# The decay table on ScalarE's DMA queue, and scores taken four chunks ahead instead of three, in a retention layer followed by two MLPs

## The chip, the cores and the metric

The kernel runs on one core of a Trainium2 chip. Its engines work side by side: TensorE (PE) multiplies matrices, VectorE (DVE) and ScalarE (ACT) work elementwise, GpSimd (POOL) does small elementwise work, SyncE (SP) issues DMA loads and stores. Each engine runs its own instructions in order and waits on semaphores for others. ACT can issue DMAs too, on a queue of its own. The metric is the device time of one execution in microseconds (us); before the change the median of 3 runs is 589.42 us (588.61 to 590.28).

## The reference

Two batches, 8 heads, 768 positions, 64 channels per head. With positions cut into blocks, a decay `lam` per head, `Dmask[i, j] = lam ** (i - j)` for i >= j and 0 otherwise:

```
for each block:
    intra = (q k^T * Dmask) v
    inter = (q * lam ** (pos + 1)) kv_state
    out   = intra + inter
    kv_state = lam ** block * kv_state + (k * lam ** (block - 1 - pos))^T v
x = out as 1536 tokens x 512
h = x @ w_in (2048 wide);  x = (max(h, 0) + alpha * min(h, 0)) @ w_out
h = x @ w_in2;             out = max(h, 0) ** 2 @ w_out2
```

All of it is f32. The reference's block is 64; the kernel uses 128, which gives the same result.

## The kernel before

**Retention.** The work is cut into 12 chunks (`NN`): 6 blocks of 128 positions by 2 batches, a chunk being one block of one batch with all 8 heads, the batches in turn. For chunk n the function names are those of the steps: `scores(n)` puts k^T q into PSUM (tile `s`); `decay(n)` multiplies it on DVE by the decay table `dec` into SBUF (`sc`); `outputs(n)` accumulates `sc` times `v` (line 459) and, from the second block on, the state times `q` (line 467) in PSUM (`o`), and makes the state's increment `pk` (line 477); `factors(n)` scales `q` by `grow` and `r` (the k rows) by `dec` on POOL; `keep_output` casts `o` to the high part `xah` on ACT; `keep_rest` makes the low part `xal`: up to chunk 8 PE subtracts the high part from `o` in PSUM (line 495) and ACT casts the rest, from chunk 9 (`RESTS`) on DVE subtracts (line 493). Only then is the `o` bank free; there are two. `keep_state` updates the state on DVE and scales it on ACT (`old`).

**The decay table.** `dec` holds, for 128 rows, 8 heads and 128 columns, powers of lam, shifted by one per row. DVE computes one strip of powers per head (`z`, 8 x 256), SP stores it to DRAM (`zd`), and a second DMA reads it back into 128 partitions with a step of one element per partition: 1024 pieces of 512 bytes. In the kernel before both DMAs are on SP's queue, and chunk 1's `v` load is held until POOL has copied one column of `dec` (line 305). `growth()` makes `grow` from the same strip with four matmuls.

**What sets the order.** All is written out by hand, and each engine runs its part in the order of the calls. Loads (`load_qk`, `load_vk`, 256 KB a tile) are issued by SP. The head takes the scores of `FIRST` = 4 chunks before any output; the first `FIRST - 2` are copied to SBUF by ACT, as `scores` has only two PSUM buffers. Between, `keep_warm` runs matmuls on zeros. Then the loop over chunks runs outputs(n), decay(n + 2), factors(n + 2), scores(n + 3) and the keeping of chunk n. DMA completion semaphores are used in turn, eight in all, so a DMA waits for the one eight places before it.

**The MLPs.** Weights come as f32 pieces of 512 KB (`raw`) and are split on ACT and DVE into a high part `wh` and a low part `wl`, a unit per piece: `start` (two ACT instructions, lines 122 and 123), `begin` (three on DVE, 129 to 131), `middle` (DVE line 139, then ACT's cast, line 141), `end` (DVE line 150). Five units run inside the retention loop (`EARLY_UNITS`), the others in the MLP's steps. A step makes `h` (line 172, 12 matmuls), activates it (`g`, high part `gh`, low part `gl`), and two steps later PE multiplies `gh` and `gl` by the second weights (line 225 or 227, 12 matmuls).

Of the kernel before, what the change touches and what calls it, by code (L numbers as in the profile page):

```python
# [7 lines left out]
F32 = mybir.dt.float32  # L8
# [7 lines left out]
B, H, S, D = 2, 8, 768, 64  # L16
CH = 128
NCH = S // CH
NN = B * NCH
NPAIR = H // 2  # L20
# [5 lines left out]
CPT = TT // CH  # L26
ZW = 256
RESTS = 9
FIRST = 4
LA = 3  # L30
DA = 2
AHEAD = 3
EARLY = 4
# [11 lines left out]
EARLY_UNITS = [0, 0, 0, 1, 0, 1, 0, 1, 0, 1, 1, 0]  # L45
# [8 lines left out]
def retention_then_two_mlps(  # L54
# [15 lines left out]
    nc = tc.nc  # L70
# [34 lines left out]
    def load_piece(queue=nc.scalar):  # L105
        if len(loaded) < 4 * NF:
            j = SEQ[len(loaded)]
            loaded.append(j)
            raws[j] = raw = rawp.tile([128, DM, 2], U32, tag="raw", name=f"raw{j}")
            w = (w1, w2)[j // (2 * NF)]  # L110
            queue.dma_start(raw.rearrange("p a b -> p (a b)"), w[j % (2 * NF)])
# [42 lines left out]
    conv = Conversion()  # L154
# [114 lines left out]
    actx = ExitStack()  # L269
    ap1 = actx.enter_context(tc.tile_pool(name="ap1", bufs=1))  # L270
    ap2 = actx.enter_context(tc.tile_pool(name="ap2", bufs=2))
    qp = actx.enter_context(tc.tile_pool(name="qp", bufs=LA + 4))
    kp = actx.enter_context(tc.tile_pool(name="kp", bufs=LA + 2))
    scp = actx.enter_context(tc.tile_pool(name="scp", bufs=LA + 1))

    psc = actx.enter_context(tc.tile_pool(name="psc", bufs=2, space=PSUM))
    pso = actx.enter_context(tc.tile_pool(name="pso", bufs=2, space=PSUM))
# [17 lines left out]
    def load_qk(n):  # L295
        q_t = qp.tile([128, NPAIR, CH], F32, tag="q", name=f"q{n}")
        k_t = kp.tile([128, NPAIR, CH], F32, tag="k", name=f"k{n}")
        nc.sync.dma_start(k_t, kt[n])
        nc.sync.dma_start(q_t, qt[n])
        qk_t[n] = q_t, k_t  # L300

    def load_vk(n):
        v_t = kp.tile([128, H, D], F32, tag="v", name=f"v{n}")
        if n == 1:
            nc.gpsimd.tensor_copy(v_t[:, 0, 0:1], dec[:, 0, 0:1])
        nc.sync.dma_start(v_t, vr[n])
        r_t = None
        if ORDER[n][0] < NCH - 1:
            r_t = kp.tile([128, H, D], F32, tag="r", name=f"r{n}")
            nc.sync.dma_start(r_t, kr[n])  # L310
        vk_t[n] = v_t, r_t
# [5 lines left out]
    def keep_warm(i):  # L317
        pw = pso.tile([128, NPAIR, CH], F32, tag="o", name=f"warm_ps{i}")
        for a in range(WARM[i]):
            nc.tensor.matmul(pw[:, a % NPAIR, :], warm, warm, start=True, stop=True)  # L320
# [20 lines left out]
        nc.gpsimd.tensor_copy(head[:, :, t], m)  # L341

    keep_warm(0)
    for n in range(FIRST):
        load_qk(n)

    nc.vector.tensor_copy(sq[:, 0:1], lam_sb)
# [8 lines left out]
    a, p = sq[:, 0 : NB - 1], sq[:, 1:NB]  # L356
# [31 lines left out]

    zd = dram.tile([H, ZW], F32, name="zd")
    dec = ap1.tile([128, H, CH], F32, name="dec")  # L390
    nc.sync.dma_start(zd, z)
    load_vk(0)
    nc.sync.dma_start(dec, bass.AP(zd[:, :].tensor, zd[:, :].offset, [[1, 128], [ZW, H], [1, CH]]))
    dec_v = dec.rearrange("p (a t) i -> p t a i", t=2)

    grow = ap1.tile([128, NPAIR, CH], F32, name="grow")

    def growth():
        pg = psk.tile([128, 2, NPAIR, D], F32, tag="pk", name="pg")
        pg = pg.rearrange("p a b c -> p (a b c)").rearrange("p (a i) -> p a i", i=CH)  # L400
        for a in range(NPAIR):
            nc.tensor.matmul(
                pg[:, a], head[:, a].rearrange("h t d -> h (t d)"), z[:, CH:ZW], start=True,
                stop=True,
            )
        nc.vector.tensor_copy(grow, pg)
# [7 lines left out]
    sc_t = {}  # L414

    def scores(n):
        q_t, k_t = qk_t[n]
        ps = psc.tile([128, 2, NPAIR, CH], F32, tag="s", name=f"s{n}")
        for a in range(NPAIR):
            for t in range(2):  # L420
                rows = slice(t * D, (t + 1) * D)
                nc.tensor.matmul(  # L422
                    ps[:, t, a, :], k_t[rows, a, :], q_t[rows, a, :], start=True, stop=True
                )
        sc = scp.tile([128, 2, NPAIR, CH], F32, tag="sc", name=f"sc{n}")
        if n < FIRST - 2:
            nc.scalar.copy(sc, ps)
            ps = sc
        sc_t[n] = sc, ps

    def decay(n):
        sc, ps = sc_t[n]
        for a in [slice(0, 2), slice(2, 4)] if n == 0 else [slice(0, 4)]:
            nc.vector.tensor_tensor(sc[:, :, a], ps[:, :, a], dec_v[:, :, a], ALU.mult)  # L434

# [14 lines left out]
    def outputs(n):  # L450
        c, b = ORDER[n]
        q_t = qk_t.pop(n)[0]
        v_t, r_t = vk_t.pop(n)
        sc = sc_t.pop(n)[0]
        po = pso.tile([128, NPAIR, CH], F32, tag="o", name=f"o{n}")

        for a in range(NPAIR):
            for t in range(2):
                nc.tensor.matmul(  # L459
                    po[t * D : (t + 1) * D, a, :], v_t[:, 2 * a + t, :], sc[:, t, a, :],  # L460
                    start=a == 0, stop=c == 0, skip_group_check=True,
                )
        if c > 0:
            for a in range(NPAIR):
                for t in range(2):
                    d = slice(t * D, (t + 1) * D)
                    nc.tensor.matmul(  # L467
                        po[d, a, :], state[b, c % 2][d, a, :], q_t[d, a, :], start=False,
                        stop=True, skip_group_check=True,
                    )  # L470
        pk = None
        if c < NCH - 1:
            pk = psk.tile([128, 2, NPAIR, D], F32, tag="pk", name=f"pk{n}")[:, 0]
            for a in range(NPAIR):
                for t in range(2):
                    h = 2 * a + t
                    nc.tensor.matmul(  # L477
                        pk[t * D : (t + 1) * D, a, :], r_t[:, h, :], v_t[:, h, :], start=a == 0,
                        stop=True, skip_group_check=True,
                    )  # L480
        return po, pk

    def keep_output(n, po):
        ti, cols = n // CPT, slice((n % CPT) * CH, (n % CPT + 1) * CH)
        xh, xl = xt[ti]
        nc.scalar.copy(xh[:, :, cols], po)

    def keep_rest(n, po):

        ti, cols = n // CPT, slice((n % CPT) * CH, (n % CPT + 1) * CH)  # L490
        xh, xl = xt[ti]
        if n >= RESTS:
            nc.vector.tensor_tensor(xl[:, :, cols], po, xh.bitcast(F32)[:, :, cols], ALU.subtract)
            return
        nc.tensor.matmul(po, less, xh[:, :, cols], start=False, stop=True, skip_group_check=True)  # L495
        nc.scalar.copy(xl[:, :, cols], po)

    def keep_state(n, pk):
        c, b = ORDER[n]
        new = state[b, (c + 1) % 2]  # L500
        if c > 0:
            nc.vector.tensor_tensor(new, pk, old_t[n], ALU.add)
        else:
            nc.scalar.copy(new, pk)
        if c < NCH - 2:
            old_t[n + B] = old = ap2.tile([128, NPAIR, D], F32, tag="old", name=f"old{n}")
            for a in range(NPAIR):
                nc.scalar.activation(
                    old[:, a, :], new[:, a, :], AF.Copy, scale=grow[:, a, CH - 1 : CH]
                )  # L510

    for n in range(FIRST):
        scores(n)
        if n == 2:
            growth()
    keep_warm(1)
    load_vk(1)
    for n in range(2):
        factors(n)
    for n in range(DA):  # L520
        decay(n)
    for n in range(NN):
        if n + FIRST < NN:
            load_qk(n + FIRST)
        if n + 2 < NN:
            load_vk(n + 2)
        if EARLY_LOADS[n]:
            load_piece(nc.sync)
        if n == 0:
            nc.sync.dma_start(alpha_sb, alpha)  # L530
        po, pk = outputs(n)
        if n + DA < NN:
            decay(n + DA)
        if EARLY_UNITS[n]:
            conv.begin()
        keep_output(n, po)
        if pk is not None:
            keep_state(n, pk)
        if EARLY_UNITS[n]:
            conv.middle(load=False)  # L540
            conv.end()
        if n + 1 < NN and EARLY_UNITS[n + 1] or n == NN - 1:
            conv.start(conv.k)
        if n + 2 < NN:
            factors(n + 2)
        if FIRST <= n + LA < NN:
            scores(n + LA)
        keep_rest(n, po)
    actx.close()
    psum["mlp"] = ctx.enter_context(  # L550
        tc.tile_pool(name="psum", bufs=1, space=PSUM, reuse_waits="tile")
# [12 lines left out]
    for s in range(len(steps) + LAG):  # L564
        if s < len(steps):
            m, t, f, part = steps[s]
# [78 lines left out]
```

## Time and profile before

| what | value |
|---|---|
| median of 3 runs | 589.42 us |
| profiled execution | 591.76 us, its span 590.0 us |
| PE busy in the span | 578.9 us (98%) |
| DVE, ACT, POOL busy | 360.1, 296.7, 28.3 us |
| mean granted clock of PE | 0.994 of full |
| decay table, issue to landing | 9.75 to 16.19 us |
| first output matmul | 17.03 us |
| first MLP matmul | 63.49 us |

The span runs from the first to the last instruction; the execution's time is 1.8 us longer. A busy share is an average over stages with different limits: here PE is full for nearly the whole span, and what isn't full lies in the first 64 us and the last 4. The granted clock is a share of full speed (2.4 GHz); 0.5 is the lower level, 1.2 GHz.

### The profile page before, as it was taken

To read this page: it belongs to the slowest core of one execution; us is meant where nothing else is said; L and a number is where in the kernel's file an instruction comes from. 1 tells how busy PE (TensorE), PEld (TensorE's weight loads), DVE (VectorE), ACT (ScalarE), POOL (GpSimd) and SP (SyncE) were. 2 spreads that over 40 slices of the span, in tenths; PEclk is the share of its full clock that TensorE was granted. 3 is DMA by queue.
4 is the path that set the end of the run, shared out by engine and by line. 5 is a ranking of instruction groups with operands and counts; after the bars stand their busy time and mean duration, and the time that the engine had idled before them with its cause. 6 is when DMAs were issued, how large, how long until landed. Compare 5 with 4: busy or idle time off the path is not lost.

```text
span 590.0 us, 7970 instructions
## 1 busy us (share of the span) xinstructions
PE 578.9 (98%) x3069; PEld 479.9 (81%) x3069; DVE 360.1 (61%) x616; ACT 296.7 (50%) x515; POOL 28.3 (5%) x31
## 2 busy tenths in 40 slices
PE   8799899999999999999999999999999999999997
PEld 7688788888888888888888888888888888888885
DVE  4489897577578777887887787577522222222422
ACT  2476777566556766576576565555522222321220
POOL 1565000000000000000000000000000000000000
PEclk9799999999999999999999999999999999999999
DMA  6895334332436223233232132332100000400401
GB/s 215 284 390 187 107 112 142 139 108 96 167 130 213 77 103 108 96 118 108 106 111 104 41 139 74 141 107 73 73 0 1 0 1 0 143 0 1 142 1 72
DMA packets 25733, 62.39 MB, mean 106 GB/s; under 512 B 2904, under 2 KB 3936, under 8 KB 25696
## 3 DMA queue, kind: packets, MB, share of 16 engines
q1 hardware_dynamic: 17632, 32.53, 15.7%
q10 hardware_dynamic: 8064, 29.36, 14.5%
q8 instruction: 24, 0.39, 0.3%
q14 instruction: 13, 0.11, 0.1%
HBM read 52.44 MB, written 9.45 MB: 105 GB/s over the span
## 4 chain that ended last, share of the span: by engine, by line
PE 96%; DMA 2%; DVE 1%; issue 0%; DVEq 0%
PE h L172 44%; PE acc L227 22%; PE acc L225 22%; PE o L459 2%; PE o L467 2%; PE s L422 2%; PE pk L477 1%; DMA dec<-zd 1%; PE o L495 1%; DVE sc L434 0%; DMA zd<-z 0%; DMA lam_sb<-in_lam_dram 0%; DVE err L367 0%; DVE sq L349 0%; DVE ps L241 0%
## 5 line engine op out<-in xcount | busy, mean ns | idle before, releaser
L191 ACT CAST gh<-g 128x512 fp32r<-128x512 f32 x96 | 59.7, 621 | 92.6 <-DVE g L182 38.6
L182 DVE SCALAR_TENSOR_TENSOR g<-h,g 128x512 f32<-128x512 f32 x48 | 33.2, 691 | 117.3 <-ACT g L181 117.3
L181 ACT ACTIVATE g<-h 128x512 f32<-128x512 f32 x48 | 28.7, 597 | 124.9 <-PE h L172 124.9
L196 DVE TENSOR_TENSOR gl<-g,gh 128x512 fp32r<-128x512 f32 x96 | 66.5, 692 | 31.0 <-ACT gh L191 22.3
L172 PE MATMUL h<-xah,wl 128*128 128x512 f32 x192 | 74.8, 390 | 0.0
L172 PE MATMUL h<-xah,wh 128*128 128x512 f32 x192 | 74.7, 389 | 0.0
L172 PE MATMUL h<-xal,wh 128*128 128x512 f32 x192 | 74.7, 389 | 0.0
L225 PE MATMUL acc<-gh,wl 128*128 128x512 f32 x192 | 74.7, 389 | 0.0
L225 PE MATMUL acc<-gh,wh 128*128 128x512 f32 x192 | 74.7, 389 | 0.0
L225 PE MATMUL acc<-gl,wh 128*128 128x512 f32 x192 | 74.7, 389 | 0.0
L172 PE MATMUL h<-xbh,wl 128*128 128x512 f32 x192 | 74.7, 389 | 0.0
L172 PE MATMUL h<-xbl,wh 128*128 128x512 f32 x192 | 74.7, 389 | 0.0
L172 PE MATMUL h<-xbh,wh 128*128 128x512 f32 x192 | 74.7, 389 | 0.0
L227 PE MATMUL acc<-wl,gh 128*128 128x512 f32 x192 | 74.7, 389 | 0.0
L227 PE MATMUL acc<-wh,gh 128*128 128x512 f32 x192 | 74.7, 389 | 0.0
L227 PE MATMUL acc<-wh,gl 128*128 128x512 f32 x192 | 74.7, 389 | 0.0
L186 DVE SCALAR_TENSOR_TENSOR g<-h,g 128x512 f32<-128x512 f32 x42 | 29.0, 691 | 41.7 <-ACT g L185 41.6
L150 DVE TENSOR_TENSOR wl<-bits,wh 128x512 fp32r<-128x512 f32 x64 | 44.8, 699 | 3.9 <-ACT wh L141 3.8
L131 DVE SCALAR_TENSOR_TENSOR bits<-raw,bits 128x512 uint32<-128x512 uint32 x64 | 45.1, 704 | 2.2
L139 DVE CUSTOM_DVE_ANT_0 bits<-raw,bits 128x1024 uint16<-128x1024 uint16 x64 | 45.1, 705 | 0.1
L122 ACT ACTIVATE bits<-raw 128x512 f32<-128x512 f32 x64 | 43.1, 674 | 0.0
L123 ACT ACTIVATE raw<-raw 128x512 int32<-128x512 uint32 x64 | 42.8, 669 | 0.0
(81 smaller groups left out, 824.0 us busy)
## 6 DMA issues: line engine op xcount, KB each, us to landing
raw<-in_w_dram ACTq DMA_DIRECT2D x56, 512.0 KB, 3.2
ps<-sums SPq DMA_DIRECT2D x24, 256.0 KB, 3.2
sums<-p SPq DMA_DIRECT2D x20, 256.0 KB, 2.2
raw<-in_w_dram SPq DMA_DIRECT2D x8, 512.0 KB, 6.0
k<-in_kt_dram SPq DMA_DIRECT2D x12, 256.0 KB, 5.7
q<-in_qt_dram SPq DMA_DIRECT2D x12, 256.0 KB, 5.4
v<-in_vr_dram SPq DMA_DIRECT2D x12, 256.0 KB, 6.0
r<-in_kr_dram SPq DMA_DIRECT2D x10, 256.0 KB, 5.3
```

Source lines behind the costliest of these rows:

```text
L122: nc.scalar.activation(x.bitcast(F32), high.bitcast(F32), AF.Abs)
L123: nc.scalar.activation(low.bitcast(I32), low, AF.Copy, scale=2.0**-29)
L131: nc.vector.scalar_tensor_tensor(x, high, 0xC0000000, x, ALU.bitwise_and, ALU.bitwise_or)
L139: nc.vector.tensor_tensor(x.bitcast(I32), x.bitcast(I32), low.bitcast(I32), ALU.add)
L150: nc.vector.tensor_tensor(lo, x, hi.bitcast(F32), ALU.subtract)
L172: nc.tensor.matmul(ph, w[:, cols], x[:, c, :], start=c == 0 and i == 0, stop=c == NC - 1 and i == 2)
L182: nc.vector.scalar_tensor_tensor(g, ph, 0.0, g, ALU.max, ALU.mult)
L186: nc.vector.scalar_tensor_tensor(g, ph, 0.0, g, ALU.max, ALU.subtract)
L191: nc.scalar.copy(gh, g)
L196: nc.vector.tensor_tensor(gl, g, gh.bitcast(F32), ALU.subtract)
L225: nc.tensor.matmul(acc[t][i], w[:, cols], g, **flags)
L227: nc.tensor.matmul(acc[t][i], g[:, cols], w, **flags)
```

## The change

The table's DMA moves from SP's queue to ACT's: a new function `tables()` holds `growth()` and the DMA, and is called after the scores of chunk 1. SP's queue goes on behind the strip's store with v0, r0, k4, q4, v1, r1, k5, q5; POOL's copy that held v1 is gone. `FIRST` goes from 4 to 5 and `LA` from 3 to 4: the head takes five chunks' scores, the first four copied to SBUF by ACT, and the loop takes scores four chunks ahead. Buffers follow: `q` from 7 to 9, `k`, `v` and `r` from 5 to 6, `sc` from 4 to 5, and `sc` is now reserved in `decay` where ACT made no copy. In the loop, the rest of a chunk that takes no scores (chunks 0 and 8) is put off until after the next chunk's outputs; from chunk 9 on the rest stands right behind the state, ahead of the weight unit's `middle`, and in chunk 10 ahead of `begin` too.

```diff
-FIRST = 4
-LA = 3
+FIRST = 5
+LA = 4
...
     def load_vk(n):
         v_t = kp.tile([128, H, D], F32, tag="v", name=f"v{n}")
-        if n == 1:
-            nc.gpsimd.tensor_copy(v_t[:, 0, 0:1], dec[:, 0, 0:1])
         nc.sync.dma_start(v_t, vr[n])
...
+    def tables():
+
+        growth()
+        nc.scalar.dma_start(
+            dec, bass.AP(zd[:, :].tensor, zd[:, :].offset, [[1, 128], [ZW, H], [1, CH]])
+        )
+
     nc.sync.dma_start(zd, z)
     load_vk(0)
-    nc.sync.dma_start(dec, bass.AP(zd[:, :].tensor, zd[:, :].offset, [[1, 128], [ZW, H], [1, CH]]))
-    dec_v = dec.rearrange("p (a t) i -> p t a i", t=2)
+    load_qk(FIRST - 1)
+    load_vk(1)
+    load_qk(FIRST)
...
     for n in range(FIRST):
         scores(n)
-        if n == 2:
-            growth()
+        if n == 1:
+            tables()
     keep_warm(1)
-    load_vk(1)
...
         po, pk = outputs(n)
+        for x in pending:
+            keep_rest(*x)
+        pending = []
         if n + DA < NN:
             decay(n + DA)
-        if EARLY_UNITS[n]:
+        if EARLY_UNITS[n] and n < NN - 2:
             conv.begin()
         keep_output(n, po)
         if pk is not None:
             keep_state(n, pk)
+        if n >= RESTS:
+            keep_rest(n, po)
         if EARLY_UNITS[n]:
+            if n >= NN - 2:
+                conv.begin()
             conv.middle(load=False)
             conv.end()
...
         if FIRST <= n + LA < NN:
             scores(n + LA)
-        keep_rest(n, po)
+            keep_rest(n, po)
+        elif n < RESTS:
+            pending = [(n, po)]
```

The head on SP's queue, before, from the strip's store on (a name's first number is the chunk, the last a buffer):

```order
L391 DMA zd_212<-z_118 8x256
L306 DMA v0_215<-in_vr_dram 128x512
L310 DMA r0_217<-in_kr_dram 128x512
L393 DMA dec_213<-zd_212 128x8x128
L306 DMA v1_284<-in_vr_dram 128x512
L310 DMA r1_287<-in_kr_dram 128x512
L298 DMA k4_295<-in_kt_dram 128x512
L299 DMA q4_294<-in_qt_dram 128x512
```

And ACT's queue now, from the first copy of scores on:

```order
L435 COPY sc0_245<-s0_236 128x1024
L435 COPY sc1_256<-s1_247 128x1024
L394 DMA dec_213<-zd_212 128x8x128
L435 COPY sc2_274<-s2_265 128x1024
L435 COPY sc3_285<-s3_276 128x1024
```

The table's DMA has left SP's row of loads and stands on ACT between the copies of chunk 1 and chunk 2; SP's loads follow the strip's store without it.

PE now, from the table's matmuls `pg` to chunk 2's outputs; before, `s4` (the scores of chunk 4) stood behind `pk1`:

```order
L410 MATMUL pg_258<-z_118,head_134 128x128 x4
L430 MATMUL s2_265<-q2_166,k2_167 128x128 x8
L430 MATMUL s3_276<-q3_170,k3_171 128x128 x8
L430 MATMUL s4_287<-q4_219,k4_220 128x128 x8
L318 MATMUL warm_ps1_296<-warm_126 128x128 x10
L470 MATMUL o0_321<-sc0_245,v0_215 64x128 x8
L488 MATMUL pk0_330<-v0_215,r0_217 64x64 x8
L470 MATMUL o1_359<-sc1_256,v1_223 64x128 x8
L488 MATMUL pk1_368<-v1_223,r1_225 64x64 x8
L506 MATMUL o0_321<-xah0_84,less_132 128x512
L430 MATMUL s5_389<-q5_227,k5_228 128x128 x8
L506 MATMUL o1_359<-xah0_84,less_132 128x512
```

Chunk 4's scores have moved ahead of the warm-up matmuls, and chunk 0's rest behind chunk 1's outputs.

DVE at the end of the retention stage, before, from chunk 9's state on (`bits4` and `bits3` are the weight units of chunks 9 and 10):

```order
L502 TENSOR_TENSOR state1_1_224<-pk9_828,old7_734 128x256
L139 ISA bits4_791<-raw4_641,bits4_791 128x1024
L150 TENSOR_TENSOR wl4_846<-bits4_791,wh4_844 128x512
L493 TENSOR_TENSOR xal2_89<-o9_811,xah2_88 128x4x128
L129 TENSOR_SCALAR bits3_848<-bits3_848 128x512
L130 TENSOR_SCALAR bits3_848<-bits3_848 128x512
L131 SCALAR_TENSOR_TENSOR bits3_848<-raw3_760,bits3_848 128x512
L139 ISA bits3_848<-raw3_760,bits3_848 128x1024
L150 TENSOR_TENSOR wl3_879<-bits3_848,wh3_877 128x512
L493 TENSOR_TENSOR xal2_89<-o10_855,xah2_88 128x4x128
L493 TENSOR_TENSOR xal2_89<-o11_884,xah2_88 128x4x128
```

and now:

```order
L513 TENSOR_TENSOR state1_1_235<-pk9_826,old7_744 128x256
L504 TENSOR_TENSOR xal2_89<-o9_809,xah2_88 128x4x128
L139 ISA bits4_801<-raw4_654,bits4_801 128x1024
L150 TENSOR_TENSOR wl4_848<-bits4_801,wh4_846 128x512
L504 TENSOR_TENSOR xal2_89<-o10_856,xah2_88 128x4x128
L129 TENSOR_SCALAR bits3_850<-bits3_850 128x512
L130 TENSOR_SCALAR bits3_850<-bits3_850 128x512
L131 SCALAR_TENSOR_TENSOR bits3_850<-raw3_769,bits3_850 128x512
L139 ISA bits3_850<-raw3_769,bits3_850 128x1024
L150 TENSOR_TENSOR wl3_881<-bits3_850,wh3_879 128x512
L504 TENSOR_TENSOR xal2_89<-o11_885,xah2_88 128x4x128
```

Each remainder `xal2` has moved up: chunk 9's ahead of line 139, chunk 10's ahead of the whole unit of `bits3`. On PE, chunk 8's rest now stands between `pk9` and `o10`, and there are no scores in chunk 8.

## Rows read from the trace of the kernel before

**Rows 1.** The page, DMA issues: count, KB each, median us to landing.

```profile
raw<-in_w_dram ACTq DMA_DIRECT2D x56, 512.0 KB, 3.2
...
q<-in_qt_dram SPq DMA_DIRECT2D x12, 256.0 KB, 5.4
```

**Rows 2.** Windows: length, busy PE, PEld, DVE, ACT, POOL, PEclk, DMA share, GB/s.

```profile
10.00:14.00 4.00, 4.00 (x43) 3.64 (x41) 0.69 (x1) 0.00 (x0) 0.00 (x0) 1.00 0.84 231
14.00:16.00 2.00, 0.85 (x8) 0.66 (x6) 0.00 (x0) 0.00 (x0) 0.00 (x0) 1.00 0.04 7
...
17.80:24.70 6.90, 6.21 (x65) 5.53 (x67) 4.04 (x4) 3.74 (x11) 3.10 (x4) 0.51 0.96 321
...
63.50:586.10 522.60, 522.53 (x2306) 432.35 (x2304) 317.26 (x533) 265.26 (x443) 0.00 (x0) 1.00 0.25 87
```

**Rows 3.** Timeline of the head: start us, us, engine, line, tile, [idle before, releaser].

```profile
8.74 0.43 SPq L310 DMA_DIRECT2D r<-in_kr_dram  x1
8.95 1.01 ACT L427 COPY sc<-s 128x1024 f32<-128x1024 f32 x1 [1.36 <-PE s L422]
...
12.35 2.50 PE L320 MATMUL warm_ps<-warm 128*128 128x128 f32 x20
...
16.29 3.29 DVE L434 TENSOR_TENSOR sc<-sc,dec 128x512 f32<-128x512 f32 x3 [4.23 <-DMA dec<-zd]
...
17.03 0.66 PE L459 MATMUL o<-sc,v 128*64 128x128 f32 x8 [2.18 <-DVE sc L434]
...
18.50 1.12 PE L459 MATMUL o<-sc,v 128*64 128x128 f32 x8 [0.80 <-DVE sc L434]
...
25.76 1.09 PE L459 MATMUL o<-sc,v 128*64 128x128 f32 x16
```

**Rows 4.** Chain that ended last, in order of time: start us, us.

```profile
9.75 6.44 DMA dec<-zd
```

**Rows 5.** DMA of 183 to 188 us: queue's packets, MB, share; issue's landing.

```profile
q1 hardware_dynamic: 530, 0.95, 55.8%
...
raw<-in_w_dram ACTq DMA_DIRECT2D x1, 512.0 KB, 5.1
```

**Rows 6.** Timeline of PE, chunk 8 to the first MLP matmul.

```profile
50.87 1.09 PE L459 MATMUL o<-sc,v 128*64 128x128 f32 x16
51.90 1.09 PE L467 MATMUL o<-q,state 64*64 64x128 f32 x16
52.92 0.69 PE L477 MATMUL pk<-v,r 128*64 128x64 f32 x16
53.53 1.16 PE L422 MATMUL s<-q,k 64*128 64x128 f32 x16
54.63 0.51 PE L495 MATMUL o<-xah,less 128*128 128x512 f32 x1
55.06 1.09 PE L459 MATMUL o<-sc,v 128*64 128x128 f32 x16
...
61.45 1.09 PE L459 MATMUL o<-sc,v 128*64 128x128 f32 x16 [1.76 <-issue]
...
63.49 0.50 PE L172 MATMUL h<-xah,wl 128*128 128x512 f32 x1
```

**Rows 7.** Timeline of DVE around the end of the retention stage.

```profile
60.67 0.68 DVE L493 TENSOR_TENSOR xal<-o,xah 128x512 fp32r<-128x512 f32 x1
61.27 0.42 DVE L129 TENSOR_SCALAR bits<-bits 128x512 f32<-128x512 f32 x1
...
69.74 0.69 DVE L196 TENSOR_TENSOR gl<-g,gh 128x512 fp32r<-128x512 f32 x1
```

**Rows 8.** Timeline of ACT in the same stretch.

```profile
53.51 0.58 ACT L496 CAST xal<-o 128x512 fp32r<-128x512 f32 x1
...
61.05 0.57 ACT L486 CAST xah<-o 128x512 fp32r<-128x512 f32 x1
```

**Rows 9.** Timeline of PE, first use of `gl` in the MLP.

```profile
72.24 0.39 PE L225 MATMUL acc<-gl,wh 128*128 128x512 f32 x1
```

More of the change, by code (lines that the diff above doesn't have):

```diff
@@ L271, in retention_then_two_mlps @@
     ap2 = actx.enter_context(tc.tile_pool(name="ap2", bufs=2))
-    qp = actx.enter_context(tc.tile_pool(name="qp", bufs=LA + 4))
-    kp = actx.enter_context(tc.tile_pool(name="kp", bufs=LA + 2))
-    scp = actx.enter_context(tc.tile_pool(name="scp", bufs=LA + 1))
+    qp = actx.enter_context(tc.tile_pool(name="qp", bufs=FIRST + 4))
+    kp = actx.enter_context(tc.tile_pool(name="kp", bufs=FIRST + 1))
+    scp = actx.enter_context(tc.tile_pool(name="scp", bufs=FIRST))
     psc = actx.enter_context(tc.tile_pool(name="psc", bufs=2, space=PSUM))
@@ L343, in retention_then_two_mlps @@
     keep_warm(0)
-    for n in range(FIRST):
+    for n in range(FIRST - 1):
         load_qk(n)
@@ L390, in retention_then_two_mlps @@
     dec = ap1.tile([128, H, CH], F32, name="dec")
+    dec_v = dec.rearrange("p (a t) i -> p t a i", t=2)
+    def tables():
[3 more added lines that the diff above has]
+        )
     nc.sync.dma_start(zd, z)
     load_vk(0)
-    nc.sync.dma_start(dec, bass.AP(zd[:, :].tensor, zd[:, :].offset, [[1, 128], [ZW, H], [1, CH]]))
-    dec_v = dec.rearrange("p (a t) i -> p t a i", t=2)
+    load_qk(FIRST - 1)
+    load_vk(1)
+    load_qk(FIRST)
     grow = ap1.tile([128, NPAIR, CH], F32, name="grow")
@@ L424, in scores @@
                 )
-        sc = scp.tile([128, 2, NPAIR, CH], F32, tag="sc", name=f"sc{n}")
-        if n < FIRST - 2:
+        if n < FIRST - 1:
+            sc = scp.tile([128, 2, NPAIR, CH], F32, tag="sc", name=f"sc{n}")
             nc.scalar.copy(sc, ps)
             ps = sc
-        sc_t[n] = sc, ps
+        sc_t[n] = ps
     def decay(n):
-        sc, ps = sc_t[n]
+        ps = sc = sc_t[n]
+        if n >= FIRST - 1:
+            sc = scp.tile([128, 2, NPAIR, CH], F32, tag="sc", name=f"sc{n}")
+        sc_t[n] = sc
         for a in [slice(0, 2), slice(2, 4)] if n == 0 else [slice(0, 4)]:
@@ L453, in outputs @@
         v_t, r_t = vk_t.pop(n)
-        sc = sc_t.pop(n)[0]
+        sc = sc_t.pop(n)
         po = pso.tile([128, NPAIR, CH], F32, tag="o", name=f"o{n}")
@@ L521, in retention_then_two_mlps @@
         decay(n)
+    pending = []
     for n in range(NN):
-        if n + FIRST < NN:
-            load_qk(n + FIRST)
+        if n + FIRST + 1 < NN:
+            load_qk(n + FIRST + 1)
         if n + 2 < NN:
@@ L531, in retention_then_two_mlps @@
         po, pk = outputs(n)
+        for x in pending:
+            keep_rest(*x)
+        pending = []
         if n + DA < NN:
             decay(n + DA)
-        if EARLY_UNITS[n]:
+        if EARLY_UNITS[n] and n < NN - 2:
             conv.begin()
```

## The prediction

> **What bounds the kernel now.** I read four views in this order. The table of windows came first, to find where TensorE (PE) is not busy. From 63.5 us to the end of the matmuls PE is busy for 522.53 of 522.60 us [rows 2]: the two MLPs are a solid block, and the change doesn't touch them. So the time can only move in the first 63.5 us, or by PE waiting inside the block. Then the timeline and the chain of waits of the head: the chain's longest piece that isn't a matmul is the decay table `dec`, issued at 9.75 and landed 6.44 us later, at 16.19 [rows 4]. VectorE (DVE) sits 4.23 us until then, PE has run out of warm-up matmuls at 14.85, and the first `o` matmul starts at 17.03, 0.84 us behind the table; its second half waits another 0.80 us for DVE [rows 3]. The gap costs twice: in 17.8 to 24.7 us the granted clock is 0.51 of full, the 1.2 GHz level [rows 2], and chunk 2's outputs begin only at 25.76 [rows 3]. From there a chunk takes PE a steady 4.19 us with no wait, until a gap of 1.76 us ahead of chunk 11's outputs, and `h`, the first matmul of the MLP, starts at 63.49 [rows 6]. Last I looked at the rows of DVE and ScalarE (ACT) around that end: PE takes the first `gl` at 72.24 [rows 9], and DVE made it at 69.74 to 70.43 [rows 7], so there is 1.8 us of slack.
>
> **The table's new queue.** ACT is in order, and issues the table behind the copy of chunk 1's scores, which ends at 8.95 + 1.01 = 9.96 [rows 3]; before, SP issued it at 9.75. Issue costs 0.2 us, then. What matters is what it shares. Before, only v0 and r0 stood ahead of it, and nothing behind: v1's load waits for POOL's copy, itself waiting for the table. Now SP issues k4, q4 at 9.2 and 9.6 (0.43 us apart, behind r0 at 8.74 [rows 3]) and then v1, r1, k5, q5, k6, q6, v2 without a stop. No row shows two queues filled at 10 us, so I bound the landing. From below: a 512 KB load on ACT's queue alone takes 3.2 us [rows 1], 13.2 us. From above: all nine of these loads go first, 9 x 0.262 MB at the 321 GB/s of the crowded stretch is 7.3 us, and the table's own 0.52 MB at the 231 GB/s of its stretch 2.3 us [rows 2]: 19.6 us. The nearest row is the weight load that ACT issues in 183 to 188 us, where SP's queue moves 0.95 MB of older loads: 5.1 us to landing [rows 5] against 3.2 alone. It was held up by 1.9 us, about what the older loads had left to move, not by twice its own length or more. At 10 us the older loads (rest of v0 and r0, k4, q4) are at most 1.05 MB, 3.3 us by 321 GB/s; 9.96 + 3.3 + 3.2 gives 16.5, and less if v0 is partly gone. I take 16.2, as before, and keep 13.2 and 19.6.
>
> The Trainium skill ("DMA: Bandwidth & Descriptors", section on queues, rings and completion order) says that each DMA engine goes round between the queues it has work for, a packet at a time, and its rules for kernel authors say that spreading loads over SP and ACT doesn't give bandwidth. By the first the table would also share with loads issued after it, and land near the upper bound; that is the last rival below. The row at 183 us leans to the older loads alone, but there nothing was issued behind.
>
> **The head's sum.** Score matmuls of chunk 4 fill PE from q4's landing: q4 is issued at 9.6; those 1.05 MB at 321 GB/s give 12.9, about 13.4 with a little for the receipt. Then 1.10 us of scores [rows 6] and 2.50 of warm-up [rows 3] end at 17.0, so that PE has no gap before the first outputs but about 1 us at 12.4 to 13.4, and I expect the clock to hold. From the table on: 0.84 to the first output and 0.80 for DVE's second half, as before; then at full clock two `o` (1.03 each), two `pk` (0.61), one `s` (1.10), two `rest` (0.43) [rows 6], together 5.24. Chunk 2 begins at 16.19 + 0.84 + 0.80 + 5.24 = 23.1 instead of 25.76: **2.7 us gained**. ACT's two extra copies (1.01 each) lie while it is idle, and decay of chunks 2 and 3 now reads SBUF, off the path. POOL loses the little copy. r2's load is next late: SP's DMAs take their semaphores in turn, and r2's is the table's, so r2 and all loads behind it wait for the table to land. They have some 7 us until chunk 2's `pk`. Against that the loads no longer pause: in 14 to 16 us the DMA moved 7 GB/s [rows 2]; I cost the wait at nothing, and at up to 2 us if the table is late.
>
> **The tail's sum**, on the clock of before. Chunk 8 has no scores any more: 1.10 us less (they ran in the head). The gap of 1.76 goes, since the remainder of chunk 9 now stands on DVE ahead of the weight unit's middle. That makes 2.86. Two waits come instead. `o9` follows `pk8` at once, but takes chunk 7's bank, which ACT empties at 53.51 + 0.58 = 54.09, when PE could start at 53.53: 0.6. And `o10` takes chunk 8's, whose rest matmul now stands right ahead of it: 0.51 of matmul, 0.58 of cast and a little to signal, 1.2 in place of the 0.43 that the step took: 0.75 [rows 6, 8]. PE reaches `h` 1.5 us earlier. But DVE doesn't: chunk 10's unit used to begin at 61.27, and now waits behind chunk 10's remainder, so behind the cast xah10. That is at 61.05 in ACT's order [rows 8], 0.61 later now since DVE's remainder (60.67 to 61.27 [rows 7]) moved ahead of the conversion that ACT waits for: 61.66, its end 62.24, plus the remainder's 0.61: the unit begins at 62.9, 1.6 later. All that follows on DVE and ACT up to the first `gl` is back to back, so `gl` ends near 72.0 instead of 70.43. PE wants it at 72.24 - 1.5 = 70.7 and stands 1.3 us. **Tail: 0.2 us gained**, between 1.5 (the unit is not late) and -0.8 (DVE one contended instruction later).
>
> Sum: 2.7 + 0.2 = 2.9 us off the profiled execution's 591.76, 588.9. That execution is 2.34 us above the runs' median of 589.42; at the median's level this is **586.5 us**. Its own range, with the table 1 us either way and the tail's bounds, is 584.9 to 588.0.
>
> **Rivals.**
> - The tail pays: DVE's unit isn't pushed back, and the 1.3 us stand doesn't appear: 585.2. For it: DVE and ACT have idle stretches there; against it: the wait on xah10 is in the order itself. Chance 0.12.
> - The clock or the fifth scores eat the gain. q4 may land as the page's median load, 5.4 us after issue [rows 1], at 15.0; scores and warm-up then end at 18.6 and chunk 2 starts near 23.9, a gain of 1.9. But PE would have stood for 2.6 us from 12.4, more than the 2.2 us before the clock fell to 1.2 GHz. At that level the way from first output to chunk 2 took 25.76 - 17.03 = 8.73 us [rows 3], so from 17.0 nothing is gained: 589.2 with the tail's 0.2. Chance 0.25, with times of 588 to 589.5.
> - Slower: the table shares with every load that SP issues after it. One mechanism, at 10 to 19 us: decay, the factors of POOL and all outputs start late, and PE stands between 17.0 and the table. From a landing of about 18.4 on, the gap is the 2.2 us after which the clock fell. At 18.8: 18.8 + 0.84 + 8.73 = 28.4, 2.6 later than now, less 0.2: 591.8. Chance 0.18. That the change doesn't bring the table sooner at all is already in the forecast.
>
> **How the numbers follow.** Forecast 0.45, the rivals 0.12, 0.25, 0.18. A measurement of this kernel tells about 0.3% (1.8 us) from no change, so faster means below 587.7. Nearly all of the forecast, the tail rival and a small part of the second count as faster: 0.57; most of the second as the same: 0.25; the last and a little more as slower: 0.18. The range leaves a tenth at either side: 584.8 to 591.2.
>
> **What would show it.** The table's landing in the chain of waits: about 16, right if 15 to 17. The granted clock in 14 to 25 us: 1.00 throughout. Chunk 2's first output (line 470) near 23. Loads without a pause at 14 to 16. At the end: the gap before chunk 11's outputs gone, one of about 0.75 before chunk 10's, and PE standing at the first down-projection (line 225) for `gl`. The forecast is wrong if the table lands past 18, if the clock halves before 25, or if PE reaches the second MLP step without a stand.

## The result and the profile after

The changed kernel is slower: 596.0 us (median of 4 runs, 595.51 to 597.6) against 589.01 us for the kernel before (4 runs, 587.95 to 590.28). The ratio is 1.0108, with a 95% interval of 1.0075 to 1.0141. The forecast was 586.5.

| us | before | after |
|---|---|---|
| profiled execution | 591.76 | 595.93 |
| its span | 590.0 | 593.9 |
| decay table landed | 16.19 [rows 4] | 20.89 |
| first output matmul `o0` | 17.03 [rows 3] | 21.73 |
| chunk 2's outputs | 25.76 [rows 3] | 29.79 |
| `h`, first matmul of the MLP | 63.49 [rows 6] | 66.55 |

The profiled execution of before is one of its slower ones, 2.75 us above its median, so the two profiles differ by only 4.2 us where the medians differ by 7.0. Within the pair, everything is lost ahead of chunk 2: its outputs start 4.03 us later, and from there to the end of the span it takes 564.2 us before and 564.1 after.

The chain of waits of after (start us, us, what) has the table as its longest piece ahead of the MLP, as before [rows 4], but much longer, with DVE's five decay multiplications behind it:

```profile
9.65 11.24 DMA dec<-zd
...
20.99 8.37 DVE sc L445 x5
```

The timeline of after's head, PE's row (start us, us, engine, line, tile, idle before and its releaser), answers to [rows 3]:

```profile
15.02 1.16 PE L430 MATMUL s<-q,k 64*128 64x128 f32 x16 [3.31 <-DMA q<-in_qt_dram]
16.11 2.50 PE L318 MATMUL warm_ps<-warm 128*128 128x128 f32 x20
21.73 0.66 PE L470 MATMUL o<-sc,v 128*64 128x128 f32 x8 [3.12 <-DVE sc L445]
23.19 0.66 PE L470 MATMUL o<-sc,v 128*64 128x128 f32 x8 [0.81 <-DVE sc L445]
...
29.79 1.09 PE L470 MATMUL o<-sc,v 128*64 128x128 f32 x16
```

PE stands twice: 3.31 us for q4 ahead of the fifth scores, then 3.12 us for the table, after the warm-up has ended at 18.61. Windows of after (length, busy PE, PEld, DVE, ACT, POOL, PEclk, DMA share, GB/s), beside [rows 2]:

```profile
10.00:14.00 4.00, 1.71 (x32) 1.51 (x28) 0.45 (x1) 1.93 (x2) 0.00 (x0) 1.00 1.05 312
14.00:16.00 2.00, 0.98 (x16) 1.00 (x16) 0.00 (x0) 0.00 (x0) 0.00 (x0) 1.00 1.05 350
...
23.00:28.00 5.00, 4.16 (x57) 3.81 (x57) 5.00 (x4) 2.02 (x6) 5.00 (x3) 0.66 0.99 280
23.90:27.20 3.30, 2.65 (x36) 2.49 (x33) 3.30 (x2) 2.02 (x6) 3.30 (x3) 0.50 1.03 281
63.50:586.10 522.60, 522.07 (x2337) 431.67 (x2336) 318.77 (x535) 267.57 (x447) 0.00 (x0) 1.00 0.25 87
```

The loads indeed no longer pause: 350 GB/s in 14 to 16 us, where it was 7 [rows 2]. The bytes are there, but they aren't the table's. The drop to the 1.2 GHz level is still there, only later and shorter: 0.50 in 23.9 to 27.2 us, where it was 0.51 in 17.8 to 24.7 [rows 2]. DVE is busy for all of 23 to 28 us, and the chain above goes through DVE up to 29.4 (20.99 + 8.37): PE now waits for decay too. The last row shows that the MLPs are untouched.

The DMA queues of after (packets, MB, share of 16 engines; q1 is SP's, q10 ACT's) in 9 to 12, 12 to 16, 16 to 18, 18 to 20 and 20 to 21 us, where 9 to 12 has no row for q10:

```profile
q1 hardware_dynamic: 437, 0.80, 97.2%
...
q1 hardware_dynamic: 487, 0.90, 63.4%
q10 hardware_dynamic: 818, 0.42, 39.1%
...
q1 hardware_dynamic: 376, 0.68, 91.6%
q10 hardware_dynamic: 184, 0.09, 16.3%
...
q1 hardware_dynamic: 276, 0.49, 66.4%
q10 hardware_dynamic: 34, 0.02, 2.9%
...
q1 hardware_dynamic: 13, 0.02, 5.7%
q10 hardware_dynamic: 4, 0.00, 0.6%
```

This is the central reading. The table is 1024 packets of 512 bytes, 0.52 MB. None of it moves before 12 us, at least 2.3 us after its issue at 9.65. Then it gets 0.42 MB in 4 us while SP's queue gets 0.90. By 18 us 0.02 MB is left, and this little takes until 20.89. The Trainium skill ("DMA: Bandwidth & Descriptors", section on queues, rings and completion order) says that an engine goes round its queues a packet at a time. The trace agrees in so far as both queues move in the same 4 us; that the turn goes by packets it doesn't show, as 818 packets of ACT's queue went beside 487 of SP's.

That loads issued after the table were served ahead of its end is seen from v1 and q6 (timeline of SP: start us, us; then the DMA issues: KB, us to landing):

```profile
10.00 0.43 SPq L304 DMA_DIRECT2D v<-in_vr_dram  x1
14.18 0.33 SPq L299 DMA_DIRECT2D q<-in_qt_dram  x1
...
v<-in_vr_dram SPq DMA_DIRECT2D x1, 256.0 KB, 6.0
q<-in_qt_dram SPq DMA_DIRECT2D x1, 256.0 KB, 6.4
```

v1 landed at 16.0 and q6 at 20.6. They were issued 0.35 and 4.5 us after the table, which landed at 20.89.

At the other end of the stage two of the forecast's three waits are there. Timeline of PE, then DVE, of after, beside [rows 6, 7]:

```profile
62.46 1.09 PE L470 MATMUL o<-sc,v 128*64 128x128 f32 x16 [0.68 <-ACT xal L507]
...
66.55 0.50 PE L172 MATMUL h<-xah,wl 128*128 128x512 f32 x1
75.56 0.50 PE L225 MATMUL acc<-gh,wl 128*128 128x512 f32 x1 [0.54 <-ACT gh L191]
...
75.54 0.69 DVE L196 TENSOR_TENSOR gl<-g,gh 128x512 fp32r<-128x512 f32 x1
```

The gap of 1.76 us ahead of chunk 11's outputs [rows 6] is gone; 0.68 us ahead of chunk 10's outputs and 0.54 us at the first down-projection have come.

### The profile page after: what moved, and what is told of

Read it like the earlier page. It is cut to its first block, busy times and chain, and to the rows that moved or that the text cites. A ratio compares the mean times of both kernels' runs of the same rounds, so it can differ in the third digit from the quotient of the medians.

```text
span 593.9 us, 7958 instructions
## 1 busy us (share of the span) xinstructions
PE 579.0 (97%) x3069; PEld 479.4 (81%) x3069; DVE 361.6 (61%) x616; ACT 298.6 (50%) x517; POOL 30.5 (5%) x30
## 3 DMA queue, kind: packets, MB, share of 16 engines
q1 hardware_dynamic: 16592, 32.01, 15.5%
HBM read 52.44 MB, written 9.45 MB: 104 GB/s over the span
## 4 chain that ended last, share of the span: by engine, by line
PE 93%; DVE 2%; DMA 2%; ACT 2%; issue 0%; POOL 0%; POOLq 0%; DVEq 0%; ACTq 0%
PE h L172 43%; PE acc L225 22%; PE acc L227 22%; DMA dec<-zd 2%; DVE sc L445 1%; PE o L478 1%; PE o L470 1%; PE s L430 1%; PE warm_ps L318 1%; PE pk L488 1%; PE o L506 1%; ACT sc L435 0%; ACT bits L122 0%; ACT raw L123 0%; ACT xah L497 0%
## 5 line engine op out<-in xcount | busy, mean ns | idle before, releaser
L225 PEld LDWEIGHTS acc<-gh,wl 128*128 128x128 f32 x192 | 36.1, 188 | 8.4 <-ACT gh L191 1.0
```

Source lines behind the costliest of these rows:

```text
L225: nc.tensor.matmul(acc[t][i], w[:, cols], g, **flags)
```

## The experiments

Two things in the change lie ahead of the first output: the table's queue, and the fifth scores, which PE must do in order, before the warm-up and `o0`. The first theory after the result was that the queue alone does it (S in the expectations). That the fifth scores do it too (P) came up when e1 had missed the time that S gave. The two were taken apart in four kernels: the change itself (both), e1 (all of the change but the queue; "scores" below), f2 (queue only) and f3 (neither, but SP's loads issued early as in the change). Every ratio is against runs of the kernel before on the same chip, with its 95% interval; the medians of before in the three sets of runs were 589.47, 589.05 and 589.77 us.

**e1_table_on_sp**: the changed kernel, the table back on SP ahead of k4.

```
 def tables():
     growth()
-    nc.scalar.dma_start(dec, ...)
...
 load_vk(0)
+nc.sync.dma_start(dec, bass.AP(zd[:, :].tensor, ...))
 load_qk(FIRST - 1)
```

> The changed kernel with one part undone: the table's DMA goes back to SP's queue, behind v0 and r0 and ahead of k4, q4, v1, r1, k5, q5. Nothing else differs from the changed kernel. Theory S (sharing): on its own queue the table shares the DMA engines piece by piece with loads that are issued after it, 512 bytes of its own against 2048 of theirs; on the loads' queue it keeps its turn. Then it lands at 15 to 17 us as in the kernel before (16.2) instead of 20.9, chunk 2's first output starts at 22.5 to 24.5 instead of 29.8, and the time is 5 to 7 us under the changed kernel's 596, at 588 to 590. Theory B (bytes in flight): any loads issued behind the table slow it, whatever queue; then it lands at 19 or later and the time stays within 2 us of 596.

Measured: 594.62 us, 1.0093 [1.0074, 1.0111]. Timeline of PE in e1 (the table landed 7.2 us after its issue):

```profile
18.07 2.08 PE L428 MATMUL s<-q,k 64*128 64x128 f32 x16 [6.17 <-DMA q<-in_qt_dram]
20.08 3.11 PE L318 MATMUL warm_ps<-warm 128*128 128x128 f32 x20
23.12 1.09 PE L468 MATMUL o<-sc,v 128*64 128x128 f32 x16
28.04 1.09 PE L468 MATMUL o<-sc,v 128*64 128x128 f32 x16
```

The table lands in 7.2 us instead of 11.2, at 16.6, as theory S had it. But the 588 to 590 us that S gave for it don't come: almost nothing is gained. (Theory B had the time right, and the table wrong, at 19 or later.) PE now stands 6.17 us for q4, which is behind the table; the fifth scores take 2.08 us where after took 1.16, the clock having fallen meanwhile, and the warm-up 3.11 instead of 2.50. The first output comes at 23.12, later than after's 21.73, though the table had long been there. So the queue isn't all: with the table back on SP, the rest of the change costs nearly as much.

**f3_sp_s4_in_loop**: the kernel before with SP's loads issued early and without the hold on v1, table on SP, fifth scores back in the loop. **f2_act_s4_in_loop**: the same, but the table on ACT's queue, behind chunk 1's copy. The loop's loads move to `load_qk(n + FIRST + 2)` and the buffers grow to 9 and 6 in both.

```
 load_vk(0)
 nc.sync.dma_start(dec, ...)        # f3; f2: nc.scalar.dma_start at n == 1 of the scores loop
+load_qk(FIRST)
+load_vk(1)
+load_qk(FIRST + 1)
...
-    if n == 1:
-        nc.gpsimd.tensor_copy(v_t[:, 0, 0:1], dec[:, 0, 0:1])
```

> As f2_act_s4_in_loop, but with the table on SP's queue behind v0 and r0 and ahead of k4. The fourth corner: neither the sharing nor the fifth scores. P and S both: the table lands at 15 to 17, the first output 0.84 later, chunk 2 at 22 to 24, the time within 1 us of before. If the earlier loads as such are dear (theory B), the time is 2 us or more above before.

> The loads of the changed kernel (table on ACT's queue beside k4, q4, v1, r1, k5, q5, k6, q6, v2, no hold, its buffers for q, k, v, r) with four chunks' scores ahead, three in the loop and the end as in the kernel before. It leaves the sharing alone and takes the fifth scores out of PE's way. Theory S: the table lands at 19.5 to 21.5 as in the changed kernel, the first output 0.84 later, chunk 2 at 27 to 29, the time 592 to 595. Theory P alone (the whole price is the fifth scores): the first output at 17 or earlier, the time within 1 us of before.

Measured: f3 589.41 us, 1.0001 [0.9985, 1.0017]; f2 595.26 us, 1.0095 [1.0076, 1.0114]. The two differ in nothing but the table's queue, and its place with it: 5.9 us. f3 came as expected but for chunk 2, 0.3 us late; f2 is as S had it, though chunk 2 and the time are each a little beyond the range given. f3, timeline of PE (the table landed 6.3 us after its issue):

```profile
16.84 0.66 PE L460 MATMUL o<-sc,v 128*64 128x128 f32 x8 [2.01 <-DVE sc L435]
...
24.32 1.09 PE L460 MATMUL o<-sc,v 128*64 128x128 f32 x16
```

f2, the same (the table landed 10.9 us after its issue):

```profile
11.80 2.50 PE L318 MATMUL warm_ps<-warm 128*128 128x128 f32 x20
21.67 1.12 PE L459 MATMUL o<-sc,v 128*64 128x128 f32 x8 [7.38 <-DVE sc L434]
29.86 0.33 PE L459 MATMUL o<-sc,v 128*64 128x128 f32 x2
```

f2, window of 17.8 to 24.7 us (columns as above, the clock third from the end):

```profile
17.80:24.70 6.90, 2.68 (x30) 2.29 (x32) 3.77 (x3) 0.40 (x1) 3.73 (x3) 0.50 0.72 249
```

On ACT's queue the table takes 10.9 us without the fifth scores in the head, 11.2 with them, and PE here stands 7.38 us for it. The clock is at the 1.2 GHz level throughout the window. In after the same time was filled with the fifth scores, their wait and the warm-up, which ended at 18.61, so that the first output waited for the table alone, and both begin chunk 2 near 29.8. On SP's queue, ahead of the same loads, it takes 6.3, and the kernel is as fast as before. The four cells: neither 1.0001, queue 1.0095, scores 1.0093, both 1.0108. Each of the two costs nearly everything by itself, since PE waits for the later of q4's work and the table; undoing one changes less than the intervals can tell, undoing both gains all of it. The cells aren't simply parts of the change, though: in e1 the table stands ahead of q4 on SP's queue, and PE gets q4 at 18.07, in after at 15.02. The change with the loads behind q4 held back until the table has landed would show what the fifth scores are worth with both in time; it was not run.

**e3_act_with_hold**: the kernel before, only the table moved to ACT's queue, v1 still held until it lands.

```
-nc.sync.dma_start(dec, ...)
...
     scores(n)
+    if n == 1:
+        nc.scalar.dma_start(dec, ...)
```

> The kernel before with the table's DMA alone moved to ACT's queue, behind the copy of chunk 1's scores; POOL's copy still holds v1's load, so that only v0 and r0 are in flight beside it. S: it lands at 15 to 17 us and the time is within 1 us of before. Theory Q (the queue itself): a table of 1024 small pieces is slow on ACT's queue whatever is beside it; then it lands at 19 or later, and the time is 3 us or more above before.

Measured: 588.93 us, 1.0002 [0.9987, 1.0017]. e3, timeline of PE (the table landed 5.2 us after its issue):

```profile
15.94 0.66 PE L458 MATMUL o<-sc,v 128*64 128x128 f32 x8 [1.02 <-DVE sc L433]
```

ACT's queue itself isn't slow: with nothing issued behind it the table takes 5.2 us. In f2 k4 and q4 stand ahead of it besides, issued 0.7 and 0.2 us earlier, and not in e3; their 0.52 MB at the 321 GB/s of [rows 2] are an estimated 1.6 us of the 5.7 us between the two. The other 4 us or so are left for the loads issued after it on the other queue. The table in the chains of f3, f2 and e3 (start us, us):

```profile
9.70 6.29 DMA dec<-zd
...
9.93 10.90 DMA dec<-zd
...
9.87 5.22 DMA dec<-zd
```

**e2_no_hold**: the kernel before without POOL's copy that holds v1.

```
-        if n == 1:
-            nc.gpsimd.tensor_copy(v_t[:, 0, 0:1], dec[:, 0, 0:1])
```

> The kernel before with POOL's one-column copy taken out that holds v1's load until the table has landed; the table stays on SP's queue, the order of loads too. S: the loads behind it on the same queue don't overtake it: it lands at 15.5 to 17 us (16.2 before), and the time is within 1 us of before, perhaps 1 us better, as loads start 3 us earlier. B: it lands at 18.5 or later and the time is 2 to 4 us above before.

Measured: 588.61 us, 1.0003 [0.9982, 1.0024]; the table took 5.4 us and landed at 14.7, before the 15.5 to 17 that S gave; chunk 2's outputs began at 22.09. On SP's queue the loads behind the table don't hurt it, so the pause in the loads [rows 2] protected nothing there, and cost nothing either.

**f1_warm_before_s4**: e1 with the warm-up ahead of the fifth scores.

```
 for n in range(FIRST):
+    if n == FIRST - 1:
+        keep_warm(1)
     scores(n)
...
-keep_warm(1)
```

> The kernel of e1_table_on_sp (the changed kernel with the table back on SP) with the second warm-up run of PE moved from behind chunk 4's scores to ahead of them. In e1 the table landed at 16.6 and DVE was ready, but PE stood 6.2 us for q4, then ran 1.1 us of scores and 3.0 of warm-up before the first output at 23.1. Theory P (place in PE's row): what stands between the table and the outputs in e1 is that chain. Then the first output comes at about 19.2, right behind the scores, chunk 2 at 24 to 25.5 instead of 28.0, and the time is 2.5 to 3.5 us under e1's 594.6. If the price in e1 lies elsewhere (memory traffic, DVE and POOL slowing each other), the time stays within 1 us of e1.

Measured: 592.65 us, 1.0055 [1.0037, 1.0073]. f1, timeline of PE:

```profile
17.18 2.07 PE L428 MATMUL s<-q,k 64*128 64x128 f32 x16 [2.96 <-DMA q<-in_qt_dram]
19.18 1.79 PE L468 MATMUL o<-sc,v 128*64 128x128 f32 x16
24.81 1.09 PE L468 MATMUL o<-sc,v 128*64 128x128 f32 x16
...
38.03 1.16 PE L428 MATMUL s<-q,k 64*128 64x128 f32 x16 [2.13 <-issue]
```

The warm-up behind q4 was part of e1's loss: without it there, chunk 2 begins 3.2 us earlier and 2.0 us are gained (1.5 when each is taken against its own runs of before), less than the 2.5 to 3.5 expected. The fifth scores still hold `o0` back until 19.18. From chunk 2 on f1 takes 1.2 us longer than e1: PE stands 2.13 us ahead of the scores at 38.03 and 0.58 us ahead of those at 47.03, where e1 has one such stand, 1.39 us ahead of those at 49.09. What these scores wait for was not tested.

**e4_tail_only**: the kernel before with the change's order at the end of the stage.

```
-        if EARLY_UNITS[n]:
+        if EARLY_UNITS[n] and n < NN - 2:
             conv.begin()
...
+        if n >= RESTS:
+            keep_rest(n, po)
+            if n >= NN - 2:
+                conv.begin()
...
-        keep_rest(n, po)
+        if n < RESTS:
+            keep_rest(n, po)
```

> The kernel before with only the new order at the end of the retention stage: from chunk 9 on the remainder stands ahead of the weight unit's middle, in chunk 10 ahead of its begin. The prediction's tail sum: PE's gap of 1.76 us ahead of chunk 11's outputs goes, but the unit of chunk 10 begins 1.6 us later and the first gl comes at 71.4 to 72.0 on the old clock, so PE stands for about 1.5 us at the first down-projection: the time is within 0.6 us of before. If instead the unit isn't late, there is no stand and the time is 1.5 to 1.8 us under before.

Measured: 589.93 us, 1.0003 [0.9986, 1.002]. e4, timeline of PE:

```profile
57.90 1.09 PE L459 MATMUL o<-sc,v 128*64 128x128 f32 x16
59.94 0.50 PE L172 MATMUL h<-xah,wl 128*128 128x512 f32 x1
...
69.53 0.50 PE L225 MATMUL acc<-gh,wl 128*128 128x512 f32 x1 [1.13 <-ACT gh L191]
```

Chunk 11's outputs (57.90) start with no wait ahead of them, and 1.13 us of it comes back at the first down-projection, where PE didn't stand in before. The order at the end is worth nothing that these runs can tell.

**f6_longer_warm**: e2 with `WARM = 12, 16` for `12, 10`.

> The kernel of e2_no_hold (the kernel before without the hold on v1) with 16 instead of 10 matmuls in the second warm-up. PE's warm-up then ends at about 15.6, near the first output, instead of 14.1. If what parts the runs at 587.5 to 588.5 from those at 590 to 591.5 is the clock falling in that gap, all runs stay near 588 at a granted clock of 1.00, and the median is about 1 us under before. If the gap is not what the clock falls for, nothing changes (within 0.3%); if the longer warm-up is in the way of the outputs, the time is up to 1 us above before.

Measured: 588.86 us, 1.0004 [0.9987, 1.0021]. The mean clock of its runs is still anything from 0.993 to 1.0: a longer warm-up doesn't hold it.

**g1_table_first**, **g4_three_scores** and **g5_v0_early** look for a version better than both, all from e2: the table ahead of v0 and r0; three scores before the table with k3 and q3 behind it; v0 and r0 ahead of the store of the strip that the table is read from.

```
# g1
-load_vk(0)
 nc.sync.dma_start(dec, ...)
+load_vk(0)
# g4 (the head's loop loads 3, and g5's move of load_vk(0) as well)
-FIRST = 4
+FIRST = 3
 nc.sync.dma_start(dec, ...)
+load_qk(FIRST)
# g5
 for n in range(FIRST):
     load_qk(n)
+load_vk(0)
...
 nc.sync.dma_start(zd, z)
-load_vk(0)
```

> The kernel of e2_no_hold with one step moved: SP issues the table ahead of v0 and r0 instead of behind them, so 0.52 MB less have to land before it. If the time follows the start of the first output, which waits for the table, its half MB less brings the table to 13.5 to 14.5 us instead of 14.8 to 16.6, the first output to 14.8 to 15.5 (v0 comes then), chunk 2 to 20.5 to 22 instead of 22.1 to 24, and the time is 1 to 2 us under before. If r0 and POOL's factor then hold up pk0, or the table isn't earlier, the time is within 0.6 us of before.

> The other way from the change: three chunks' scores ahead of the outputs instead of four, from the kernel of e2_no_hold. k3 and q3 are loaded behind the table, v0 and r0 ahead of the strip's store, and chunk 3's scores run behind pk0. The table lands at 13 to 14.5, the first output 0.84 later, chunk 2 with one more set of scores (1.1 us) ahead of it at 21 to 22.5, the time 0.5 to 2 us under before. If the strip's store is held up behind v0 and r0, the table lands at 15 or later and the time is within 0.6 us of before or up to 1 us above.

> The kernel of e2_no_hold with v0 and r0 issued right behind k3 and q3, ahead of the strip's store, while SP would otherwise wait for DVE. The bytes ahead of the table are the same, but they start some 3 us earlier and fill a part of the time in which the DMA engines idle at 8.5 to 10. If that idle time counts, the table lands at 13.5 to 15 and the time is 0.5 to 1.5 us under before; if the store waits behind the loads instead, it lands at 15.5 or later and the time is within 0.6 us of before or above.

Measured: g1 589.66 us, 0.9998 [0.9979, 1.0017]; g4 589.11, 0.9985 [0.9964, 1.0005]; g5 588.06, 0.998 [0.9963, 0.9997]. g1, timeline of PE:

```profile
18.49 0.82 PE L475 MATMUL pk<-v,r 128*64 128x64 f32 x16 [1.39 <-POOL r L442]
```

g4, the same:

```profile
21.55 1.09 PE L458 MATMUL o<-sc,v 128*64 128x128 f32 x16
...
58.30 1.63 PE L458 MATMUL o<-sc,v 128*64 128x128 f32 x16 [1.79 <-issue]
```

The window of 8 to 10 us, of the kernel before:

```profile
8.00:10.00 2.00, 1.83 (x32) 1.67 (x30) 0.00 (x0) 1.01 (x1) 0.00 (x0) 1.00 0.66 207
```

and of g5:

```profile
8.00:10.00 2.00, 1.78 (x25) 1.47 (x22) 0.00 (x0) 1.34 (x2) 0.00 (x0) 1.00 0.87 332
```

In g1 the table lands at 14.95 (9.45 + 5.5), no earlier than e2's 14.73, and PE then waits 1.39 us for POOL's factors. g4 has the earliest chunk 2 of all (21.55) and loses it afterwards: from there to the end takes 566.9 us against e2's 563.6. The gap at 58.30 is 1.79 us, where e2 has 1.25, and behind it the granted clock of g4 falls to the 1.2 GHz level (window of 58.7 to 62.1 us), which in e2 it doesn't there:

```profile
58.70:62.10 3.40, 3.40 (x30) 2.74 (x27) 2.54 (x5) 0.85 (x2) 0.00 (x0) 0.50 0.18 52
```

From chunk 2 to `h` g4 takes 40.2 us and e2 37.4, so most of what g4 loses lies in this stage. g5 fills a stretch that moved 207 GB/s before with 332. It is the only version whose interval lies below 1, by 0.2%, which is less than the 0.3% that this measurement was taken to tell; and in the traces its table (14.98) and chunk 2 (22.35) come no earlier than e2's (14.73 and 22.09).

## Why the prediction was wrong

- **The table's landing, 16.2 with bounds 13.2 and 19.6: failed, and first in the sum.** It landed at 20.89, outside the bounds. The step that failed took the table to wait only for older loads, from a weight load that took 5.1 us [rows 5] behind which nothing was issued, as the prediction itself noted. e3 comes nearest to that for the table, and gave 5.2 us; with the change's loads in flight f2 gave 10.9. The row was the wrong neighbour. The upper bound, all nine loads ahead of the table, was 1.3 us short. It left out what v0 and r0 still had to move: from 9.65 to 20.9 us SP's queue moved 2.81 MB in after, not the nine loads' 2.36, and the 0.45 MB more are an estimated 1.4 us at the same 321 GB/s.
- **q4 at 13.4, warm-up done at 17.0, clock held: failed.** q4 landed at 15.0, the median of [rows 1], which the second rival had used; PE stood 3.31 us, not 1. The clock held through this first stand, and halved around 24 us, after the second. The prediction let q4's lateness only eat the gain. That the fifth scores and the warm-up stand ahead of `o0` in PE's order, so that q4 becomes a condition for the first output just as the table is, was named but not priced as a loss. In after it cost nothing yet, as the table came 2.3 us behind the warm-up's end; in e1, with the table in time and q4 behind it, the change still loses 5.2 us.
- **Table to chunk 2, 0.84 + 0.80 + 5.24: the first two right, the third not.** The rows of after give 0.84 (20.89 to 21.73) and 0.81; what is left of the way from the table to chunk 2 (20.89 to 29.79) is 7.25 us where the sum had 5.24, with a granted clock of 0.50 in 23.9 to 27.2. Part of that is DVE. "Off the path" was wrong for the decay that now reads SBUF. Operations on the table in after (engine, operation, tile, count: ns min/median/max):

```profile
L455 POOL TENSOR_TENSOR r<-r,dec x10: 1059/1164/2037, 21.0 to 50.3; 128x512 f32<-128x512 f32 x10
L445 DVE TENSOR_TENSOR sc<-s,dec x8: 1208/1211/1215, 29.3 to 59.2; 128x1024 f32<-128x1024 f32 x8
L445 DVE TENSOR_TENSOR sc<-sc,dec x5: 691/2075/2284, 21.0 to 27.3; 128x1024 f32<-128x1024 f32 x3, 128x512 f32<-128x512 f32 x2
```

  From PSUM (`s`) a whole chunk takes 1.21 us, from SBUF (`sc`) up to 2.28, while POOL multiplies too. Two more of these ran in the head, and the chain has DVE for 8.37 us.
- **r2 behind the table: right.** It was issued at 20.90, as the table landed; no wait for it stands on the chain.
- **The tail, 0.2 gained: right in the sum, in part by luck.** From chunk 2's outputs to `h` took 36.76 us instead of 37.73 (0.97 gained, 1.5 forecast), and PE then stood 0.54 (1.3 forecast), for `gh` from ACT and not for `gl`. Of the two waits in the sum, the one ahead of chunk 10 came (0.68 for 0.75) and the 0.6 ahead of chunk 9 didn't; instead PE stood 0.82 and 0.27 us ahead of the scores at 41.70 and 50.42, which no term had. From chunk 2 to the end of the span 0.1 us was gained; e4 alone shows no change in time either. The rival that the tail pays is refuted.
- **From 588.9 to 586.5: not borne out.** The sum took 2.34 us off because the profile of before stood above its median, as if that of after would too. It stood at it: 595.93 us against 596.0.
- **The rivals.** The last one, that the table shares with all loads behind it, is what happened. It had 0.18 and 591.8 us. Its landing of 18.8 was 2.1 us early, and it took its 2.6 us of loss from a chunk 2 at 25.76, where e2, e3, e4 and f3, which cost nothing, have 22.1 to 24.3.

What stays open: how the turn between the queues is shared out (only packets and bytes per stretch were read), why the last 0.02 MB of the table took so long, what f1's scores wait for behind chunk 2, why g4's clock falls late, and what the fifth scores would be worth with the table and q4 both in time.

## What to carry to other kernels

A load moved to a second queue doesn't only leave the line it stood in, it loses its place ahead of everything issued after it; keep a load that all engines wait for first in the busy queue, or hold back what follows. In an in-order engine, work pulled ahead to fill a wait makes its own inputs a condition for all that stands behind it: ask when these land before calling it filler. When a trace is to tell how two queues share, pick a stretch where both still have loads to issue, not one where the other is running dry.

## What the runs showed of the hardware

- A 0.52 MB table of 512-byte rows lands 4.3 to 7.2 us after issue on SP's queue (g4, e1), 5.2 on ACT's with nothing issued behind, and 10.9 to 11.2 on ACT's beside a filled SP queue (f2, after). Its first bytes then move 2.3 us or more after issue, and v1 and q6, issued after it on the other queue, land ahead of it (16.0 and 20.6 against 20.89).
- DVE's multiplication of 128x1024 takes 1.21 us with its input from PSUM and up to 2.28 us from SBUF beside POOL's, whose 128x512 one goes from 1.06 to 2.04.
- The clock doesn't follow the length of PE's stand alone: after 3.31 us in after the fifth scores took 1.16 us, after 2.96 us in f1 2.07. Runs of one and the same kernel differ by it as well: of the kernel before's, nine with a mean clock of 0.993 or 0.994 take 590.6 to 592.2 us; fifty with 0.999 or 1.000 have a median of 588.8, but reach from 586.7 to 591.5, so the clock isn't all.
